# An mLSTM cell and a multiplicative feed-forward block: the third group's output tiles as two pairs by seven products, and other places for folded sums and kept halves

## The chip, the cores and the metric

The kernel runs on one core of a Trainium2 chip. The metric is the device time of one execution in microseconds (us). The engines are named as the profile names them: PE (TensorE; PEld is its weight load), DVE (VectorE), ACT (ScalarE), POOL (GpSimd) and SP (SyncE, whose queue issues most DMAs; ACT's queue issues the output DMAs).

## What is computed

The first block is a recurrent cell. For every batch (4), head (8) and time step (768) a 40 x 40 state is decayed, gets an outer product of v and k, and is read with q:

```
C = f_stab * C + i_stab * outer(v_t, k_t);   n = f_stab * n + i_stab * k_t
y_t = sigmoid(o_t) * (C q_t) / max(|n . q_t|, 1)
```

Its output, put in rows of 320 (8 heads x 40) for 3072 tokens, is x of the second block:

```
h = ((x @ w1) * (x @ w2)) @ w3        # w1, w2: 320 x 1024, w3: 1024 x 1024
out = h @ w_out                        # w_out: 1024 x 320
```

All is float32.

## The kernel before, in words

w3 and w_out are folded: the kernel computes `w3o = w3 @ w_out` once (`w3_mm`), so that a token needs two up products (x w1 and x w2), their elementwise product `ab` (1024 long), and one down product `ab @ w3o`. The raw w3 pieces are made into float32 in buffers `w3` (`convert`, L249), turned, and multiplied with `wo`, which holds w_out. After the last `w3_mm` (step 16) the words of `wo` are free.

The work is cut into 24 units of 128 time steps of one batch (NU = 24), and the main loop runs steps s = 0 to 31. Step s does the cell of unit s (`quarter_work`, s <= 24): PE's records `cell<-v_all,pw`, `cell<-state,qT`, `cell<-qT,kT`, `cell<-vw,kbuf`, in two accumulator tiles `cell[0]` and `cell[1]` (L75), each of two banks. DVE, ACT and POOL make the unit's rows y out of it (DVE L427 to L454, ACT L434, POOL L332, L310 and the state's decay L337). Four units make a group of 512 tokens; there are six groups, 0 to 5.

- Up products of groups 0 to 2 are made plainly (`up`, `up_rest`, steps 2 to 15) into two `ab` tiles per group, out of a rotating pool of six.
- Up products of groups 3 to 5 are made in twelve "late blocks" (`up_by_seven`, one a step, steps 19 to 30): a 2 x 2 product by seven multiplications instead of eight. Its order is `single` and `shared` (PE records `pa`, `pb`, then banks p15 and p67, which in steps 19 to 24 are `cell[1]` and `cell[0]`), later `left` (`pa<-xT,wr`, ahead of the cell's own matmuls), later `product`. ACT empties p15 into four "kept" quarters for each of the two factors j (L710, L712), DVE adds p67 to them (L692, L694, 256 columns each), POOL adds two and two of them (L719), then DVE adds the four blocks `pa`, `pb` to the kept quarters (L692, L694, 512 columns each) and POOL multiplies the factors into `ab` (L737). The kept quarters lie in `wo` (`aside`, L657). The last block does POOL's part on DVE.
- Down products are made in two ways. `ffn_out` makes one tile of 128 tokens whole: 8 matmuls of 320 columns, one ACT copy into `o_sb` (L749), one DMA (L751). `out_by_seven` makes a pair of tiles by seven products of 160 columns with 4 matmuls each (28), in four accumulators o15, o67, o23, o4; it needs sums of the weights, T1 to T4 (`out_weight_sums`, L761, on POOL), and sums of `ab`, S1 to S4 (`ab_sums`, L776, on DVE), and puts the products together with ACT (L798, L800) and DVE (L805 to L811). A matmul in float32 leaves two records in the profile.

The order of the down products is a list written out by hand: group 0's tiles 0 and 1 whole in step 16; the pairs (0,1) and (1,0) in step 17 and (1,1) in step 18 (`pairs_by`); group 2's four tiles whole, one in each of steps 19 to 22; group 3's first two tiles whole in steps 23 and 24; all other pairs (3,1) to (5,1) from step 27 on (`n_out`). In steps 19 to 24 a whole tile is accumulated in `cell[1]`, after `shared` and before `left`. The weight sums T are made twice: at step 16 into `wo`, for the pairs of steps 17 and 18, and again in steps 24 and 25 into `v_all`, `gates` and `q_all`, since the kept quarters overwrite them in `wo` in between.

PE's order is the order in which the program issues matmuls (`in_order`, L84). The other engines run their instructions in the order of issue; the tile framework adds the waits between engines from what each instruction reads and writes.

Of the kernel before, what the change touches and what calls it, by code (L numbers as in the profile page):

```python
# [8 lines left out]
FP = mybir.dt.float32  # L9
U32 = mybir.dt.uint32  # L10
AF = mybir.ActivationFunctionType
OP = mybir.AluOpType
# [4 lines left out]
def kernel(  # L17
# [212 lines left out]


    w3T_t = {}
    turned_w3, ready_w3 = [], []
# [5 lines left out]
    def convert():  # L239
        if not scaled:  # L240
            scale_next()
        dst, raw, ko, half = scaled.pop(0)
        if dst is not None:
            to_f32(dst, raw, nc.vector if dst.shape[-1] == CW else nc.gpsimd)
            return
        w3 = wst.tile([128, CW], FP, name="w3", tag="w3")
        to_f32(w3, raw, nc.vector)
        if half == 0:
            w3T_t[ko] = wst.tile([128, FO, 128], FP, name="w3T", tag="w3T")  # L249
        nc.vector.transpose(out=w3T_t[ko].rearrange("c k (m r) -> c m k r", r=32)[:, 2 * half:2 * half + 2],  # L250
                            in_=w3.rearrange("r (m c k) -> r m k c", m=2, k=FO))
        if half:
            turned_w3.append(ko)
# [369 lines left out]

    ab_t = {}

    def up(gr, fs, cs):


        if gr not in ab_t:
            ab_t[gr] = [ffn.tile([128, FO, 2 * P], FP, name="ab", tag="ab", bufs=6) for _ in range(2)]  # L630
        x, n = x_t[gr], cs.stop - cs.start
        pa, pb = mps([128, len(fs), n], "pa"), mps([128, len(fs), n], "pb")
        for p, wt in ((pa, w1), (pb, w2)):
            for i, f in enumerate(fs):
                for cc in range(KF):
                    mm(p[:, i, :], wt[:, cc, f * 128:(f + 1) * 128], x[:, cc, cs], start=(i == cc == 0), stop=False)
        return pa, pb, x, gr, fs, cs
# [18 lines left out]
    S_t, T_t = {}, {}  # L656
    aside = wo.rearrange("p f d -> p (f d)")  # L657

# [17 lines left out]
    def up_by_seven(gr, f, bank, aside_by):  # L676
# [3 lines left out]
        (B11, B12), (B21, B22) = ([x[:, cc, i * TH:(i + 1) * TH] for i in range(2)] for cc in range(KF))  # L680
        block, kept = {}, [aside[:, j * 4 * TH:(j + 1) * 4 * TH].rearrange("p (i t) -> p i t", i=4) for j in range(2)]
        lo, hi = (ffn.tile([128, 2, TH], FP, name="a_sb", tag="a_sb") for _ in range(2))
# [20 lines left out]
        def shared():  # L703
            p15, p67 = [bank(2 + j) for j in range(2)], [bank(j) for j in range(2)]
            for j in range(2):
                mm(p15[j][:, 0], of(j, 0, 0), B11, stop=False)
                mm(p15[j][:, 1], sum_of(j, 0), T[0], start=False)
            for j in range(2):
                if j:
                    nc.scalar.copy(out=kept[j][:, 0:4:3], in_=p15[j])  # L710
                else:
                    nc.scalar.mul(out=kept[j][:, 0:4:3], in_=p15[j], mul=UP ** -2)  # L712
            for j in range(2):
                mm(p67[j][:, 0], sum_of(j, 1), T[1], stop=False)
                mm(p67[j][:, 1], sum_of(j, 2), T[2], start=False)
            for j in range(2):
                for i in range(2):
                    add(j, kept[j][:, 1 + i], p67[j][:, i], kept[j][:, i])
                aside_by.tensor_tensor(out=kept[j][:, 1:4:2], in0=kept[j][:, 1:3],  # L719
                                        in1=kept[j][:, 3:4].to_broadcast([128, 2, TH]), op=OP.add)  # L720

        def left():
            if gr not in ab_t:
                ab_t[gr] = [ffn.tile([128, FO, TH], FP, name="ab", tag="ab", bufs=6) for _ in range(2)]
            for t in range(2):
                for i in range(2):
                    for j, e in quarters:
                        c0 = (f + i * FH) * 128 + e * L
                        mm(block[j][t][halves[e], i], wr[halves[j], c0:c0 + L], x[halves[j], KF, t * TH:(t + 1) * TH],
                           start=False, stop=(i == 1))  # L730
            for j, dst in enumerate(((lo, hi), [t[:, f:FO:FH, :] for t in ab_t[gr]])):
                add(j, dst[0], block[j][0], kept[j][:, 0:3:2])
                add(j, dst[1], block[j][1], kept[j][:, 1:4:2])

# [20 lines left out]

    def out_weight_sums(places):

        (B11, B12), (B21, B22) = ([w3o[:, k * KH:(k + 1) * KH, i * NH:(i + 1) * NH] for i in range(2)] for k in range(2))
        T1, T2, T3, T4 = T_o[:] = [m[:, i * KH * NH:(i + 1) * KH * NH].rearrange("p (f n) -> p f n", n=NH) for m, i in places]
        for dst, p, q in ((T1, B12, B11), (T2, B22, T1), (T3, B22, B12), (T4, B21, T2)):  # L760
            yield nc.gpsimd.tensor_tensor(out=dst, in0=p, in1=q, op=OP.subtract)  # L761

    T_o, S_o = [], {}
    wsums = out_weight_sums(((v_all, 0), (gates, 0), (gates, 1), (q_all, 0)))

    def quarters_of_ab(gr, j):
        return [[ab_t[gr][j][:, k * KH:(k + 1) * KH, t * P:(t + 1) * P] for k in range(2)] for t in range(2)]

    def ab_sums(gr, j, mem=None):
        mem = mem or [t.rearrange("p h d -> p (h d)") if j == 0 else io.tile([P, H, L], FP, name="pw", tag="pw", bufs=5)  # L770
# [3 lines left out]
        for dst, p, q, op in ((S1, A21, A22, OP.add), (S2, S1, A11, OP.subtract), (S3, A11, A21, OP.subtract),  # L774
                              (S4, A12, S2, OP.subtract)):
            nc.vector.tensor_tensor(out=dst, in0=p, in1=q, op=op)  # L776

    def out_by_seven(gr, j, rows=None):

# [9 lines left out]
        def products(pairs, name):  # L789
            po = mps([P, len(pairs), NH], name)  # L790
            for i, (a, b) in enumerate(pairs):
# [3 lines left out]

        p15 = products(((A11, B11), (S1, T1)), "o15")
        if whole:
            nc.scalar.copy(out=o2[:, 0:4:3], in_=p15)  # L798
        for i in () if whole else range(2):
            nc.scalar.copy(out=o[3 * i], in_=p15[:, i])  # L800
        p67 = products(((S2, T2), (S3, T3)), "o67")
        p23 = products(((A12, B21), (S4, B22)), "o23")
        p4 = products(((A22, T4),), "o4")
        for i in range(2):
            nc.vector.tensor_tensor(out=o[1 + i], in0=p67[:, i], in1=o[i], op=OP.add)  # L805
        if whole:
            nc.vector.tensor_tensor(out=o2[:, 1:4:2], in0=o2[:, 1:3], in1=o2[:, 3:4].to_broadcast([P, 2, NH]), op=OP.add)
        for p, q in () if whole else ((1, 1), (3, 2)):
            nc.vector.tensor_tensor(out=o[p], in0=o[q], in1=o[3], op=OP.add)
        nc.vector.tensor_tensor(out=rows[0], in0=p23.rearrange("p i n -> p (i n)"), in1=rows[0], op=OP.add)  # L810
        nc.vector.tensor_tensor(out=o[2], in0=p4[:, 0], in1=o[2], op=OP.add)  # L811
        for t in range(2):
            t0 = (2 * j + t) * S + gr * P
            leaving.append((out[t0:t0 + P, :], rows[t]))
        if whole:
            leave()

    leaving = []

    def leave():  # L820
        while leaving:
# [4 lines left out]
           for f in range(0, FO, 2)]  # L826
    downs = [(0, 0), (0, 1)] + [(2, j) for j in range(GT)] + [(3, 0), (3, 1)]
    pairs_by = {17: [(0, 1), (1, 0)], 18: [(1, 1)]}
# [4 lines left out]
    n_seven = [0] * 19 + [1] * 12 + [0]  # L833
    n_down = [0] * 16 + [2] + [0] * 2 + [1] * 6 + [0] * 7
    n_out = [0] * 27 + [1, 0, 1, 0, 3]
# [8 lines left out]
    for s in range(len(n_up)):  # L844
# [35 lines left out]
        if s == 16:  # L880
            for _ in out_weight_sums([(aside, i) for i in range(4)]):
                pass
            ab_sums(0, 1, [ffn.tile([128, 2, TH], FP, name="a_sb", tag="a_sb").rearrange("p i t -> p (i t)") for _ in range(2)] +
                    [wst.tile([128, CW], FP, name="w3", tag="w3") for _ in range(2)])
        if s == 17:
# [5 lines left out]
        for x in pairs_by.get(s, ()):  # L891
            if x == (1, 0):
                mem = ffn.tile([128, FO, TH], FP, name="ab", tag="ab", bufs=6)
                ab_sums(1, 1, [mem[:, i * 2:i * 2 + 2].rearrange("p i t -> p (i t)") for i in range(4)])
            out_by_seven(*x, [wst.tile([128, CW], FP, name="w3", tag="w3")[:, 0:DM] if x == (1, 0) else
                              ffn.tile([P, DM], FP, name="o_sb", tag="o_sb", bufs=2) for _ in range(2)])
        if s >= len(n_up) - 2:
            ab_sums(*summed.pop(0))
        def pairs():
            for i in range(n_out[s]):  # L900
                out_by_seven(*outs.pop(0))
                if summed and n_out[s] > 1:
# [11 lines left out]
        if NY < s < NU and s not in pairs_by:  # L914
            if s < NU - 1:
                weights(s + 1)
            out_gate(s)
        if seven and s <= NU:
            ffn_out([downs.pop(0) for _ in range(n_down[s])], [cell[1][:, i, 0:DM] for i in range(2)])
# [53 lines left out]
        with tc.issue_after(gated.ins) if gated else nullcontext():  # L973
            if seven:
                seven[3]()
            for _ in range({NU: 1, NU + 1: 3}.get(s, 0)):
                next(wsums)
            if s == NU + 1:
# [98 lines left out]
```

## Time and profile before

| | us |
|---|---|
| runs of the kernel (3) | 419.91, 423.56, 425.32; median 423.56 |
| the profiled execution | 419.57, of which span 417.7 |
| PE busy | 407.5 |
| DVE busy | 311.5 |
| ACT busy | 182.9 |
| POOL busy | 183.3 |

Busy times by stretch of the profiled execution, from the windows of the trace:

| stretch (us) | steps | PE | DVE | ACT | POOL |
|---|---|---|---|---|---|
| 213.7 to 231.3 | pairs of 17 | 17.60 | 14.46 | 6.47 | 5.02 |
| 231.3 to 242.8 | 18 | 11.50 | 9.40 | 5.18 | 6.28 |
| 242.8 to 256.9 | 19 | 14.10 | 9.62 | 6.12 | 5.80 |
| 256.9 to 271.1 | 20 | 14.20 | 10.82 | 6.22 | 8.40 |
| 271.1 to 285.2 | 21 | 14.10 | 10.65 | 6.22 | 7.88 |
| 285.2 to 299.3 | 22 | 14.10 | 12.08 | 6.21 | 7.89 |
| 326.8 to 351.5 | 25 to 27 | 24.22 | 22.94 | 3.84 | 18.62 |

How to read the lines: the page gives each engine's busy time and share, and 40 equal slices whose digit is the busy share in tenths (PEclk: the clock granted to PE). A timeline line is the start, the duration, engine, line of the kernel, operation, what is written from what, shapes, how often; a bracket gives the idle time ahead and what ended it. A line of waits gives the waiting instruction, what it waited for, the sum, how often, and the longest. Lines of the chain are start, duration and what ran.

### The profile page before, as it was taken

The page shows a single profiled execution, that of the slowest core. Times are in us where ns is not written, and L with a number is a line of the kernel's source. Part 1 is how long each engine was busy: PE and PEld are TensorE (multiplying, and loading weights), DVE is VectorE, ACT ScalarE, POOL GpSimd, SP SyncE. Part 2 cuts the span into 40 slices and gives each one's busy share as a digit, 9 for nine tenths or more (in the row PEclk, how much of TensorE's full clock was granted, in tenths as well). Part 3 has the DMA queues.
Part 4 walks back from the last instruction along what each step waited for, and adds up shares of the span by engine and source line. Part 5 has one row for each costly group of instructions (what it writes and reads, how often), then busy time and mean ns, then how long its engine had stood idle before and what let it go on. Part 6 is the DMA issues. An engine that isn't in the chain of part 4 may idle for free.

```text
span 417.7 us, 13157 instructions
## 1 busy us (share of the span) xinstructions
PE 407.5 (98%) x5351; PEld 337.3 (81%) x5351; DVE 311.5 (75%) x587; ACT 182.9 (44%) x526; POOL 183.3 (44%) x237
## 2 busy tenths in 40 slices
PE   7999899999999989999999999999999999999997
PEld 4768688888788877888789988778778778888896
DVE  6767967668977856869889786778875798575971
ACT  4787756558643844843842452354312211111000
POOL 4533773442302302308971443765544496642100
PEclk9999999999999999999999999999999999999999
DMA  8989987788995584843415487753221010000001
GB/s 189 229 158 193 196 192 128 176 186 182 203 198 140 97 188 130 153 94 61 92 47 118 121 156 148 126 107 82 53 54 39 33 24 31 2 2 31 2 33 63
DMA packets 125291, 46.56 MB, mean 111 GB/s; under 512 B 104816, under 2 KB 116400, under 8 KB 125232
## 3 DMA queue, kind: packets, MB, share of 16 engines
q1 hardware_dynamic: 121632, 41.70, 49.5%
q10 hardware_dynamic: 3600, 4.03, 2.8%
q8 instruction: 42, 0.69, 0.7%
q14 instruction: 17, 0.14, 0.1%
HBM read 39.91 MB, written 5.80 MB: 109 GB/s over the span
## 4 chain that ended last, share of the span: by engine, by line
PE 85%; DVE 4%; DMA 3%; SPq 3%; issue 2%; ACT 1%; POOL 0%; DVEq 0%; ACTq 0%; POOLq 0%
PE pa L92 21%; PE cell L92 20%; PE pb L92 14%; PE o L92 14%; PE wp L92 8%; PE p L92 3%; PE po L92 2%; DMA o_in<-in_o_gate_dram 2%; DMA w3o<-in_moe_w_dram 1%; SPq L136 1%; SPq L186 1%; PE px L95 1%; PE pt L95 1%; DVE pw L776 1%; DVE ab L692 1%
## 5 line engine op out<-in xcount | busy, mean ns | idle before, releaser
L337 POOL TENSOR_TENSOR state<-state,decay 128x164 f32<-128x164 f32 x40 | 22.4, 561 | 118.7 <-DVE state L406 97.5
L92 PE MATMUL pa<-xT,w 128*128 128x256 f32 x240 | 60.6, 383 | 0.0
L92 PEld LDWEIGHTS pa<-xT,w 128*128 128x128 f32 x240 | 44.4, 190 | 6.6 <-POOL w L202 0.4
L305 ACT ACTIVATE pw<-pw,aT 128x64 f32<-128x64 f32 x184 | 46.4, 337 | 2.7 <-DVE pw L297 1.9
L92 PE MATMUL pb<-xT,w 128*128 128x256 f32 x192 | 45.9, 381 | 1.1 <-POOL w L202 1.0
L92 PEld LDWEIGHTS pb<-xT,w 128*128 128x128 f32 x192 | 36.3, 190 | 7.0 <-POOL w L202 2.3
L737 POOL TENSOR_TENSOR ab<-ab,a_sb 128x512 f32<-128x512 f32 x22 | 29.4, 1356 | 27.3 <-DVE ab L692 27.3
L647 DVE TENSOR_TENSOR ab<-pb,a_sb 128x512 f32<-128x512 f32 x24 | 16.5, 690 | 32.2 <-ACT a_sb L646 32.0
L719 POOL TENSOR_TENSOR wo<-wo 128x512 f32<-128x512 f32 x22 | 27.4, 1269 | 28.8 <-DVE wo L694 28.8
L92 PE MATMUL pa<-xT,wr 64*64 64x256 f32 x384 | 37.0, 386 | 0.2 <-POOL wr L202 0.2
L92 PE MATMUL pb<-xT,wr 64*64 64x256 f32 x384 | 36.4, 380 | 0.0
L646 ACT ACTIVATE a_sb<-pa 128x512 f32<-128x512 f32 x24 | 14.3, 595 | 49.7 <-PE pb L92 49.7
L310 POOL TENSOR_SCALAR_AFFINE_SELECT pw<-pw 64x512 f32<-64x512 f32 x48 | 33.3, 694 | 5.9 <-ACT pw L305 4.3
L92 PE MATMUL wp<-wo,w3T 128*128 128x320 f32 x128 | 35.6, 433 | 0.0
L434 ACT COPY h<-cell 64x164 f32<-64x164 f32 x56 | 16.2, 289 | 41.3 <-DVE y L427 40.8
L92 PEld LDWEIGHTS pa<-xT,wr 64*64 64x64 f32 x384 | 18.9, 132 | 15.1 <-issue 8.4
L92 PEld LDWEIGHTS wp<-wo,w3T 128*128 128x128 f32 x128 | 23.8, 190 | 9.0
L92 PE MATMUL cell<-w3o,ab 128*128 128x320 f32 x96 | 26.8, 432 | 0.0
L694 DVE SCALAR_TENSOR_TENSOR a_sb<-pa,wo 128x512 f32<-128x512 f32 x12 | 8.3, 690 | 22.7 <-PE pa L92 22.7
L92 PEld LDWEIGHTS cell<-w3o,ab 128*128 128x128 f32 x96 | 18.3, 190 | 6.9
L92 PEld LDWEIGHTS pb<-xT,wr 64*64 64x64 f32 x384 | 20.1, 133 | 3.0
L92 PE MATMUL o<-w3o,ab 128*128 128x160 f32 x136 | 21.5, 302 | 0.5 <-DVE wo L694 0.5
(222 smaller groups left out, 935.9 us busy)
## 6 DMA issues: line engine op xcount, KB each, us to landing
raw<-in_moe_w_dram SPq DMA_DIRECT2D x64, 128.0 KB, 3.3
kbuf<-in_k_dram SPq DMA_DIRECT2D x24, 160.0 KB, 4.8
v_all<-in_v_dram SPq DMA_DIRECT2D x24, 160.0 KB, 4.5
o_in<-in_o_gate_dram SPq DMA_DIRECT2D x24, 160.0 KB, 4.9
pw<-U_d SPq DMA_DIRECT2D x28, 128.0 KB, 3.9
raw<-in_moe_w_out_dram SPq DMA_DIRECT2D x8, 320.0 KB, 5.0
out_dram<-o_sb ACTq DMA_DIRECT2D x12, 160.0 KB, 3.9
yb<-y_d SPq DMA_DIRECT2D x36, 48.0 KB, 2.9
```

The lines of the kernel that those rows point to most:

```text
L92: in_order(nc.tensor.matmul(out, lhsT=lhsT, rhs=rhs, start=start, stop=stop))
L95: in_order(nc.tensor.transpose(out, in_, ident[0:n, 0:n]))
L136: nc.sync.dma_start(out=dst, in_=rows(src, n))
L305: nc.scalar.activation(out=pw[:, h, :], in_=src[:, h, :], func=AF.Exp, bias=aT[:, c, b * H + h:b * H + h + 1])
L310: nc.gpsimd.affine_select(out=pw[r], in_=pw[r], compare_op=OP.is_ge, fill=0.0, base=0, pattern=[[0, H], [1, L]], channel_multiplier=-1)
L337: nc.gpsimd.tensor_tensor(out=new, in0=old, op=OP.mult, in1=decay[:, b * NP:(b + 1) * NP, 2 * c + x:2 * c + x + 1] .to_broadcast([P, NP, D1]))
L434: nc.scalar.copy(out=h[halves[x], 0:H // 2] if x == e else h[halves[x], H // 2:H], in_=ph[x][halves[e]])
L646: nc.scalar.mul(out=a_sb, in_=pa, mul=UP ** -2)
L647: nc.vector.tensor_tensor(out=ab_t[gr][j][:, fs[0]:fs[-1] + 1, t0:t0 + a_sb.shape[-1]], in0=pb, in1=a_sb, op=OP.mult)
L694: nc.vector.scalar_tensor_tensor(out=out, in0=p, scalar=UP ** -2, in1=q, op0=OP.mult, op1=OP.add)
L719: aside_by.tensor_tensor(out=kept[j][:, 1:4:2], in0=kept[j][:, 1:3], in1=kept[j][:, 3:4].to_broadcast([128, 2, TH]), op=OP.add)
L737: aside_by.tensor_tensor(out=t[:, f:FO:FH, :], in0=t[:, f:FO:FH, :], in1=a, op=OP.mult)
```

## The change

1. The weight sums T1 to T4 are made once, at step 16, into `wo`, and stay there. The second making (four POOL instructions in steps 24 and 25) is gone.
2. The kept quarters of the first factor lie in the two former `w3` buffers, now one tile `w3_mem`; those of the second factor lie in the rows of `ab` in which the block ends, and are overwritten in place. ACT's copy of the second factor's p15 becomes two copies of 256 columns, and POOL's two kept sums of 512 columns become four of 256.
3. The six `ab` tiles are fixed: groups 0 to 5 use (0,1), (2,3), (4,5), (2,3), (4,1), (5,0).
4. Group 2's four whole tiles become the pairs (2,0) and (2,1) by seven products, each in two halves: o15 and o67 in steps 19 and 21, o23 and o4 in steps 20 and 22, in the banks of `cell[1]`, where the whole tile was. The DVE sums of a half stand after DVE's adds of p67 and ahead of `left`'s sums.
5. The S sums of (2,0) and (1,1) are made on POOL in step 17 after the pair (0,1) (those of (1,1) were made on DVE), in the tiles of group 0; those of (2,1) on POOL in step 19.

```diff
+    w3_mem = wst.tile([128, 2 * CW], FP, name="w3", tag="w3", bufs=1)
...
-        w3 = wst.tile([128, CW], FP, name="w3", tag="w3")
+        w3 = w3_mem[:, half * CW:(half + 1) * CW]
...
+    ab_mem = [ffn.tile([128, FO, 2 * P], FP, name=f"ab{i}", tag=f"ab{i}", bufs=1) for i in range(6)]
+    ab_t = {gr: [ab_mem[i] for i in of] for gr, of in enumerate(((0, 1), (2, 3), (4, 5), (2, 3), (4, 1), (5, 0)))}
...
+        kept = [[w3_mem[:, i * TH:(i + 1) * TH] for i in range(4)],
+                [ab_t[gr][i % 2][:, f + i // 2 * FH] for i in range(4)]]
...
-            for j in range(2):
-                if j:
-                    nc.scalar.copy(out=kept[j][:, 0:4:3], in_=p15[j])
-                else:
-                    nc.scalar.mul(out=kept[j][:, 0:4:3], in_=p15[j], mul=UP ** -2)
+            nc.scalar.mul(out=w3_mem.rearrange("p (i t) -> p i t", i=4)[:, 0:4:3], in_=p15[0], mul=UP ** -2)
+            for i in range(2):
+                nc.scalar.copy(out=kept[1][3 * i], in_=p15[1][:, i])
...
-                aside_by.tensor_tensor(out=kept[j][:, 1:4:2], in0=kept[j][:, 1:3],
-                                        in1=kept[j][:, 3:4].to_broadcast([128, 2, TH]), op=OP.add)
+                for p, q in ((1, 1), (3, 2)):
+                    aside_by.tensor_tensor(out=kept[j][p], in0=kept[j][q], in1=kept[j][3], op=OP.add)
...
-            for j, dst in enumerate(((lo, hi), [t[:, f:FO:FH, :] for t in ab_t[gr]])):
-                add(j, dst[0], block[j][0], kept[j][:, 0:3:2])
-                add(j, dst[1], block[j][1], kept[j][:, 1:4:2])
+            at = [[w3_mem.rearrange("p (i t) -> p i t", i=4)[:, t:4:2] for t in range(2)],
+                  [ab[:, f:FO:FH, :] for ab in ab_t[gr]]]
+            for j, dst in enumerate(((lo, hi), at[1])):
+                for t in range(2):
+                    add(j, dst[t], block[j][t], at[j][t])
...
-wsums = out_weight_sums(((v_all, 0), (gates, 0), (gates, 1), (q_all, 0)))
...
-    def out_by_seven(gr, j, rows=None):
+    def out_by_seven(gr, j, rows=None, bank=None):
...
+        if bank:
+            yield first_sums(first())
+            yield second_sums(*second())
+        else:
+            p67 = first()
+            p23, p4 = second()
+            first_sums(p67)
+            yield second_sums(p23, p4)
...
-    downs = [(0, 0), (0, 1)] + [(2, j) for j in range(GT)] + [(3, 0), (3, 1)]
+    downs = [(0, 0), (0, 1), (3, 0), (3, 1)]
...
-    n_down = [0] * 16 + [2] + [0] * 2 + [1] * 6 + [0] * 7
+    n_down = [0] * 16 + [2] + [0] * 6 + [1] * 2 + [0] * 7
...
+            if x == (0, 1):
+                ab_sums(2, 0, in_ab(1), nc.gpsimd)
+                ab_sums(1, 1, in_ab(0), nc.gpsimd)
...
+        if s in (19, 21):
+            halved = out_by_seven(2, (s - 19) // 2, [out_row() for _ in range(2)], lambda name: cell[1][:, int(name in ("o67", "o4")), 0:DM]
+                                  .rearrange("p (i n) -> p i n", n=NH))
+        if s in range(19, 23):
+            next(halved)
+        if s == 19:
+            ab_sums(2, 1, in_ab(0), nc.gpsimd)
...
-            for _ in range({NU: 1, NU + 1: 3}.get(s, 0)):
-                next(wsums)
```

In the new `out_by_seven`, `first()` issues o15, ACT's copies and o67; `second()` issues o23 and o4; `first_sums` is the former L805 to L809, `second_sums` the former L810 and L811 and the row's two DMAs, which leave at the end of the step.

## The prediction

> **What bounds the kernel now.** First the page's busy table and its 40 slices:
> ```profile
> span 417.7 us, 13157 instructions
> PE 407.5 (98%) x5351; PEld 337.3 (81%) x5351; DVE 311.5 (75%) x587; ACT 182.9 (44%) x526; POOL 183.3 (44%) x237
> PE   7999899999999989999999999999999999999997
> PEclk9999999999999999999999999999999999999999
> ```
> TensorE (PE) is busy 98% of the span at full clock. So time comes off by issuing less PE work, and goes back on wherever PE waits for a bank of accumulators. Second, PE's own waits: in the late part there is one above 0.2 us.
> ```profile
> PE o L92 <- DVE wo L694: 0.5, 1, 0.5
> ```
> Third, PE's timeline, for the price of both ways to make output tiles: step 16 (two tiles whole), step 17 (pairs by seven products), step 22 (one tile):
> ```profile
> 204.95 8.78 PE L92 MATMUL po<-w3o,ab 128*128 128x320 f32 x32
> 215.91 1.25 PE L92 MATMUL o<-w3o,ab 128*128 128x160 f32 x8
> 217.00 2.34 PE L92 MATMUL o<-wo,a_sb 128*128 128x160 f32 x16
> 291.36 4.47 PE L92 MATMUL cell<-w3o,ab 128*128 128x320 f32 x16
> ```
> The chain of waits, which merges such runs, says it without the pipelined tail:
> ```profile
> 205.12 8.61 PE po L92 x32
> 233.16 7.80 PE o L92 x56
> 371.41 7.61 PE o L92 x56
> ```
> Two tiles whole take 8.61 to 8.62 us (32 records of 0.269), a pair by seven takes 7.61 (56 of 0.136). Halving the columns halves the time of a record, so seven products in place of eight pay in full. Fourth, the timelines of DVE and POOL where the change puts work:
> ```profile
> 293.98 0.42 DVE L674 TENSOR_TENSOR w3T<-xT,w3T 128x256 f32<-128x256 f32 x1
> 294.31 0.88 DVE L694 SCALAR_TENSOR_TENSOR wo<-cell,wo 128x256 f32<-128x256 f32 x2
> 296.97 0.69 DVE L694 SCALAR_TENSOR_TENSOR a_sb<-pa,wo 128x512 f32<-128x512 f32 x1 [0.99 <-PE pa L92]
> 301.39 0.67 DVE L447 TENSOR_TENSOR h<-y,h 128x328 f32<-128x328 f32 x1 [0.66 <-ACT h L434]
> 235.45 0.64 POOL L337 TENSOR_TENSOR state<-state,decay 128x164 f32<-128x164 f32 x1 [14.10 <-DVE state L406]
> 240.64 0.81 POOL L674 TENSOR_TENSOR w3T<-xT,w3T 128x256 f32<-128x256 f32 x1
> 340.53 2.03 DVE L776 TENSOR_TENSOR pw<-ab 128x512 f32<-128x512 f32 x1
> ```
> The bracket is the idle time ahead. In step 22 DVE rests only 0.99 us before its block sums; POOL stands idle 14.10 us in step 17; L776, 0.69 us when alone, takes 2.03 beside POOL's L761; and L447, 0.50 when alone, takes 0.67 beside L737.
>
> **The change, part by part.** Durations are of the one profiled execution: 419.57 us, span 417.7. It lies 3.99 under the median of the runs, 423.56, so I add that difference at the end.
>
> *Third group as two pairs.* Out go four tiles of 16 records, 4 x 4.31 = 17.24 us; in come 2 x 56 records, 2 x 7.61 = 15.22. Gain 2.02 us, on PE, which is the path. By steps: 19 and 21 keep their length (32 x 0.136 = 4.35 for 4.31), 20 and 22 lose 1.05 us (24 x 0.136 = 3.26).
>
> *Second set of folded weight sums.* Four L761 on POOL go (1.79 + 2.00 + 1.99 + 1.99 = 7.8 us, at 329.9 and 340.0 to 345.9). POOL is off the path, but the last two hold L776 of 340.53 and 342.48 at 2.03 instead of 0.69: 2.7 us on DVE just ahead of the L694 at 347.24 that PE waits for at 348.17. Against that, the third block sum now overwrites what POOL's four kept sums read, so at 336.35 DVE waits for all four, to about 334.43 + 3.0 = 337.4: 1.05 later. Net 1.6 us earlier, so the 0.48 us wait goes: gain 0.48. Next late there is nothing; PE runs on without a gap.
>
> *Kept halves.* Per late block ACT copies 2 x 256 columns for one of 512. An estimate from the copy of 160 columns (0.23) and of 512 (0.58) is 0.3 each, so 0.1 more. In steps 19 to 22 they end about 0.2 after p67 may begin, and PE reaches cell[1][1] only two microseconds later, with o67: nothing. POOL does four sums of 256 for two of 512. The nearest row, L674 on POOL, is 0.73 to 0.81: four spanned 3.0 us, for 2.49. The kept sums for left() are ready 0.5 later; at 295.3 + 3.0 = 298.3 they still meet the third block sum, which began at 298.44. Nothing on PE.
>
> *Sums of (2,0), (1,1) in step 17, on POOL.* They wait for the last read of (0,1)'s tile, about 223.6. Eight at the rows L667 (same shape, 1.27 to 1.72, mean 1.43) end at 235.0, before L337 can start at 235.45. Queued behind are that state, vw, the masks and the token sums, which end at 241.45 with T4 read by PE at 243.30: 1.85 us of slack. At 1.72 each the eight end at 237.4, 1.9 late, and PE loses 0.1. I take 0, the mean being nearest. DVE loses four L776 here (2.61 us).
>
> *Sums of (2,1) in step 19, on POOL.* They stand after the kept sums, 251.3 + 3.0 = 254.3, and take 4 x 1.43 = 5.7, to 260.0. Behind them waits L337 for DVE's state at 260.12: just in time. But they run beside the new DVE sums, next.
>
> *New sums on DVE, before left()'s sums.* First half: two L805 (0.68) and two L809 (0.69 alone, 1.15 beside POOL at 240.47); second half: L810 (0.48) and L811 (0.32). PE's cell matmuls now wait for these to empty cell[1], where ACT did it in 0.42.
> - Step 19: o67 ends near 253.4; 0.68 and 1.15 put the first L694 at 255.3 for 254.46. PE needs its bank at 256.91, has it at 256.0; the chain through L427 and ACT's h ends 0.6 later, against 0.5 to 1.0 of slack at p15. Bounds 0 and 1.2 (both L809 waiting out a POOL sum of 1.36); I take 0.3.
> - Step 20: PE is 1.05 us earlier and POOL's kept sums, which were late already (266.10), end at 269.1 to 269.6; the third block sum still ends before PE wants the bank at 271.4. Step 21 like 19, beside shorter POOL sums. Together 0 to 0.6; I take 0.1.
> - Step 22: the kept adds end at 295.99, behind four token sums L674. L810 and L811 follow to 296.8, later if step 21 left DVE behind (0.5 us). Before, cell matmuls began at 297.53; now they are due at about 296.4. PE waits 0.4 to 0.9; bounds 0 and 1.4; I take 0.7.
>
> *Queues.* Two output DMAs of a pair leave from ACT's queue at the ends of steps 20 and 22, behind the h copies, instead of one in each of four steps. The row buffers are next written two steps later and the landing took 3.9 us: nothing. SP's order does not change, and cutting the pairs into steps adds no instruction. The last block's kept sums move from two L719 on DVE (0.69 each) to four of 256 (0.42): 0.3 us in a stretch where PE's next operands are made 3 us ahead.
>
> *Sum.* -2.02 - 0.48 + 0.3 + 0.1 + 0.7 = -1.4 us, so 418.2 for an execution like the profiled one, and 422.2 beside the median. All waits at their lower bounds give -2.5 (421.1), at the upper ones -2.5 + 1.2 + 0.6 + 1.4 + 0.1 = +0.8 (424.4).
>
> **One rule weighed.** L776 at 2.03 beside a POOL instruction of 1.99, but L447 at only 0.67 for 0.50 beside L737, say that DVE sums from SBUF sometimes wait out a POOL instruction and sometimes hardly lose. The Trainium skill's page "SBUF — State Buffer", section "SBUF: two separate sides", is stricter: a DVE operation with two SBUF inputs and a GpSimd operation reading SBUF take an exclusive lock on shared ports for a whole instruction, and the loser blocks fully. By that rule the third rival below would be the forecast; the row of L776 agrees, that of L447 does not clearly.
>
> **The rivals.**
> 1. *All sums hidden* (421.1): for it, DVE rests 2.0 to 2.5 us before its block sums in steps 19 to 21; against it, 0.99 in step 22 while PE's stretch there shrinks by 1.05.
> 2. *DVE sets the pace of steps 19 to 22* (slower). Place: PE's first cell matmul of each step, waiting for the pair's sums behind the kept adds. Price, if nothing is hidden: 2 x (0.68 + 1.15) + 2 x 0.80 = 5.3 us, against 2.5 gained: +2.8, or 426.4. It decides once these waits pass 2.5 us together. For it: DVE is busy 10.6 to 12.1 of 14.1 us in these steps. Against: three of them have rest to spare.
> 3. *The lock bites*: each two-input DVE sum in steps 19 and 21 waits out a POOL sum. Step 19 then costs 1.2, step 21 0.5, with 0.7 in 22 and 0.1 in 20: 2.5 together, so 423.6, no change.
> 4. *POOL late into step 18*: at L761's 2.0 each the eight sums end at 239.6, 4.2 late, PE waits 2.3 for T4: -1.4 + 2.3 = +0.9, or 424.5. Against: L761 has 640 columns, not 512.
> 5. *The change does not shorten PE's work*: if each short record took its weight load's 0.190 us, a pair would be 10.6 and the whole 2 x (10.6 - 8.62) = +4.0, less 0.48: 427.1. The pairs of steps 17 and 18 rule it out nearly.
>
> **How the numbers follow.** Forecast 0.50, all hidden 0.17, DVE's pace 0.10, the lock 0.15, POOL late 0.05, no shortening 0.03. Cases of both signs are near each other; the forecast's own range is 421.1 to 424.4. The runs of one kernel spread from 419.91 to 425.32, 3.7 below and 1.8 above their median, which widens that to 417.4 and 426.2; the slower rival at 426.4 is let in: 417.5 to 427. A measurement of this kernel tells about 2% (8.5 us) from no change; no case reaches it, so faster 0.02, same 0.92, slower 0.06, the small ones for what I have not seen.
>
> **What would show it.** Right: PE's cell records for the third group number 56 per pair in 7.6 us; no L761 after step 16; no PE wait at the o products of step 27; PE waiting for the o_sb sums in step 22 for under 1 us. Wrong: PE waits on o_sb sums in all four steps (rival 2), a wait for w3T at step 19's start (rival 4), or L809 in step 19 near 1.3 each (rival 3).

## The result and the profile after

The changed kernel takes 425.82 us (median of 22 runs, 423.50 to 429.51); the kernel before, in the same rounds, 421.18 (22 runs, 418.63 to 425.32). The ratio is 1.0117, 95% interval 1.009 to 1.0144: 1.2% slower, inside the 2% but clear of 1. The prediction was 0.3% faster (-1.4 us); its own range ended at +0.8, and only three of its rivals, with chances of 0.10, 0.05 and 0.03, lay beyond that. The profiled execution took 423.62 us, 4.05 more than that of before. Ratios, here and below, leave out executions in a slow state: one of run e5, one of run e7 and two of the kernel before in those rounds.

The page of the kernel after, busy times and slices:

```profile
span 421.9 us, 13293 instructions
PE 407.7 (97%) x5399; PEld 340.4 (81%) x5399; DVE 315.9 (75%) x597; ACT 183.3 (43%) x538; POOL 197.8 (47%) x267
PE   7999899999999999999998999999999999999997
PEclk9999999999999999999999999999999999999999
```

PE is idle for 14.2 us of the span where it was idle for 10.2: the loss is waiting. Its busy time is as before (407.5) although the change takes work away, as PE is busy longer, too, in the steps with waits: from 216.67 to 236.27 us, the step 17 of the table below, for 17.70 us, in the same step before for 17.18. POOL has 14.5 us more to do. One slice of PE in the middle, the 22nd, fell below 9. PE's waits, kernel after, from 196 to 335 us, give the places (before there was none in these steps, and one of 0.5 us later, at the o products of step 27):

```profile
PE o L92 <- DVE o_sb L807: 1.9, 1, 1.9
PE cell L92 <- ACT o_sb L799: 1.2, 2, 0.6
PE cell L92 <- issue: 0.9, 1, 0.9
PE cell L92 <- ACT h L435: 0.6, 1, 0.6
PE cell L92 <- DVE state L417: 0.3, 1, 0.3
```

The wait of 0.5 is gone, as foreseen; five others have come. (The one for `issue` is in a stage before the change's.) To size them I take a step's length as the time between the first PE records of it and of the next, from PE's timeline. A step begins with its feed-forward products and ends with its cell matmuls; the last column runs from step 25 to the end of PE's last record.

| kernel | 17 | 18 | 19 | 20 | 21 | 22 | 23 | 24 | after 24 |
|---|---|---|---|---|---|---|---|---|---|
| before | 17.18 | 9.68 | 14.14 | 14.16 | 14.14 | 14.13 | 14.14 | 13.34 | 87.82 |
| after | 19.60 | 9.68 | 15.20 | 14.49 | 15.02 | 13.52 | 14.23 | 13.35 | 87.07 |
| difference | +2.42 | 0 | +1.06 | +0.33 | +0.88 | -0.61 | +0.09 | +0.01 | -0.75 |

Step 17 began 0.76 us later (216.67 for 215.91); in the runs below its start scatters from 214.7 to 218.6 us. With that, this is the 4.2 us of span.

**Step 17.** The timelines of POOL and DVE, kernel after, while (0,1) and (1,0) are multiplied:

```profile
222.07 1.90 POOL L774 TENSOR_TENSOR ab<-ab 128x512 f32<-128x512 f32 x1
222.15 0.69 DVE L774 TENSOR_TENSOR xT<-ab 128x512 f32<-128x512 f32 x1
222.88 1.64 DVE L774 TENSOR_TENSOR xT<-xT,ab 128x512 f32<-128x512 f32 x1
224.05 1.60 POOL L774 TENSOR_TENSOR ab<-ab,ab 128x512 f32<-128x512 f32 x1
224.45 1.76 DVE L774 TENSOR_TENSOR xT<-ab 128x512 f32<-128x512 f32 x1
225.62 1.71 POOL L774 TENSOR_TENSOR ab<-ab 128x512 f32<-128x512 f32 x1
226.13 1.75 DVE L774 TENSOR_TENSOR w3T<-ab,xT 128x512 f32<-128x512 f32 x1
227.29 1.71 POOL L774 TENSOR_TENSOR ab<-ab,ab 128x512 f32<-128x512 f32 x1
227.80 0.67 DVE L807 TENSOR_TENSOR o_sb<-o,o_sb 128x160 f32<-128x160 f32 x2
```

POOL's sums of (2,0) begin at 222.07, while PE is still at work on (0,1). Three of DVE's four sums of (1,0) take 1.64 to 1.76 us for the 0.69 of the first. They stand ahead of L807, which empties the bank that PE wants next; it starts at 227.80, and PE has stood still for 1.90 us when it goes on:

```profile
228.52 2.44 PE L92 MATMUL o<-wo,xT 128*128 128x160 f32 x16 [1.90 <-DVE o_sb L807]
```

The step is 2.42 us longer: 1.90 of idle time and 0.52 more of busy time. Before, L805 (now L807) stood at 223.93 and there was no gap:

```profile
223.33 0.69 DVE L776 TENSOR_TENSOR w3T<-ab,xT 128x512 f32<-128x512 f32 x1
223.93 0.68 DVE L805 TENSOR_TENSOR o_sb<-o,o_sb 128x160 f32<-128x160 f32 x2
224.61 3.42 PE L92 MATMUL o<-wo,xT 128*128 128x160 f32 x24
```

**Steps 19 to 22.** PE's timeline of the first half of (2,0) in step 19 and the second in step 20, kernel after, with the bracket of idle time:

```profile
252.09 1.25 PE L92 MATMUL cell<-w3o,ab 128*128 128x160 f32 x8
253.18 1.25 PE L92 MATMUL cell<-wo,ab 128*128 128x160 f32 x8
255.01 2.44 PE L92 MATMUL cell<-wo,ab 128*128 128x160 f32 x16 [0.58 <-ACT o_sb L799]
```

```profile
268.70 2.34 PE L92 MATMUL cell<-w3o,ab 128*128 128x160 f32 x16
270.88 1.25 PE L92 MATMUL cell<-wo,ab 128*128 128x160 f32 x8
```

The work came out as forecast: 32 records, then 24, in place of two tiles of 16 wide ones. But o67 waits for ACT's two copies of o15, although it writes the other bank of the cell tile. And DVE's sums beside POOL, in step 19:

```profile
257.69 1.28 POOL L774 TENSOR_TENSOR ab<-ab 128x512 f32<-128x512 f32 x1
258.26 2.24 DVE L811 TENSOR_TENSOR o_sb<-o_sb 128x160 f32<-128x160 f32 x2
259.04 1.28 POOL L774 TENSOR_TENSOR ab<-ab,ab 128x512 f32<-128x512 f32 x1
260.42 0.68 DVE L695 SCALAR_TENSOR_TENSOR a_sb<-pa,w 128x512 f32<-128x512 f32 x1
```

Two small sums take 2.24 us, and behind them the block sums L695 and, further on, the operands h and state of step 20 come late (0.6 and 0.3 us in the list of waits). L695, which reads PSUM, takes 0.68 beside the same POOL sums.

The granted clock matters to the median: in the profiled execution it was 1.0, but 17 of the 22 executions show a mean of 0.996 or less. Those 17 have a median of 426.04, the other five one of 424.43.

### The profile page after: what moved, and what is told of

Its sections match the earlier page's. It is cut to its first block, busy times and chain, and to the rows that moved or that the text cites. A ratio compares the mean times of both kernels' runs of the same rounds, so it can differ in the third digit from the quotient of the medians.

```text
span 421.9 us, 13293 instructions
## 1 busy us (share of the span) xinstructions
PE 407.7 (97%) x5399; PEld 340.4 (81%) x5399; DVE 315.9 (75%) x597; ACT 183.3 (43%) x538; POOL 197.8 (47%) x267
## 4 chain that ended last, share of the span: by engine, by line
PE 82%; issue 4%; SPq 4%; POOL 3%; DVE 3%; DMA 3%; ACT 1%; POOLq 0%; DVEq 0%; ACTq 0%
PE pa L92 21%; PE cell L92 17%; PE pb L92 14%; PE o L92 12%; PE wp L92 8%; PE p L92 5%; DMA w3o<-in_moe_w_dram 3%; SPq L136 2%; POOL wo L760 1%; PE px L95 1%; SPq L186 1%; POOL ab L774 1%; PE pt L95 1%; PE po L92 1%; DVE xT L774 1%
## 5 line engine op out<-in xcount | busy, mean ns | idle before, releaser
L719 POOL TENSOR_TENSOR w<-w 128x256 f32<-128x256 f32 x22 | 16.0, 728 | 34.0 <-DVE w L695 30.3
L333 POOL TENSOR_TENSOR vw<-v_all,wT 128x328 f32<-128x328 f32 x24 | 18.6, 777 | 7.0 <-DMA v_all<-in_v_dram 5.3
L92 PEld LDWEIGHTS o<-w3o,ab 128*128 128x128 f32 x136 | 19.3, 190 | 1.1 <-issue 0.8
L695 DVE SCALAR_TENSOR_TENSOR a_sb<-pa,w 128x512 f32<-128x512 f32 x12 | 8.2, 687 | 15.0 <-PE pa L92 14.5
```

Of the source, the lines that this page charges most:

```text
L92: in_order(nc.tensor.matmul(out, lhsT=lhsT, rhs=rhs, start=start, stop=stop))
L333: nc.gpsimd.tensor_tensor(out=vw_t[n], in0=vbuf[n % NBV], op=OP.mult, in1=wT[:, c, b * H:(b + 1) * H].unsqueeze(2).to_broadcast([P, H, D1]))
L719: aside_by.tensor_tensor(out=kept[j][p], in0=kept[j][q], in1=kept[j][3], op=OP.add)
```

## Experiments

Theory A: the loss is (1) POOL's sums of (2,0) beside DVE's sums of (1,0) in step 17, (2) o67's wait for ACT's copies in steps 19 and 21, (3) POOL's sums of (2,1) beside L811 in step 19; the kept halves and the single set of weight sums cost nothing. Rivals are named with each run. Step lengths of all runs, in us:

| run | 17 | 18 | 19 | 20 | 21 | 22 | 23 | 24 | after 24 |
|---|---|---|---|---|---|---|---|---|---|
| e1_kept_only | 17.18 | 9.67 | 14.15 | 14.16 | 14.13 | 14.14 | 14.13 | 13.35 | 87.07 |
| e2_reversed | 17.18 | 9.67 | 15.03 | 14.07 | 15.01 | 13.53 | 14.22 | 13.35 | 87.07 |
| e3_copy_after | 22.02 | 9.67 | 14.68 | 14.49 | 14.17 | 13.94 | 14.23 | 13.34 | 87.07 |
| e4_no_sums_21 | 20.67 | 9.67 | 15.03 | 13.12 | 15.02 | 13.47 | 14.23 | 13.35 | 87.07 |
| e5_reversed_and_copy_after | 17.18 | 9.67 | 14.68 | 14.49 | 14.17 | 13.93 | 14.22 | 13.34 | 87.07 |
| e6_sums_21_on_dve | 17.18 | 9.68 | 14.41 | 14.42 | 14.17 | 13.96 | 14.22 | 13.34 | 87.07 |
| e7b_sums_21_in_two_halves | 17.18 | 9.68 | 14.18 | 13.58 | 14.17 | 14.45 | 14.22 | 13.34 | 87.07 |
| e8_sums_l811_later | 17.17 | 9.68 | 14.18 | 14.85 | 14.27 | 14.08 | 14.23 | 13.35 | 87.07 |
| e9_token_sums_later | 17.18 | 9.68 | 14.18 | 13.52 | 14.26 | 13.78 | 14.96 | 13.35 | 87.07 |
| e10_filler_in_the_wait | 19.60 | 9.68 | 15.29 | 14.48 | 15.02 | 13.47 | 14.22 | 13.35 | 87.07 |

**The first two parts alone.** Kept halves and single weight sums as in the change; the third group whole, and the sums of (1,1) on DVE, as before.

```diff
-    downs = [(0, 0), (0, 1), (3, 0), (3, 1)]
+    downs = [(0, 0), (0, 1)] + [(2, j) for j in range(GT)] + [(3, 0), (3, 1)]
...
-            if x == (0, 1):
-                ab_sums(2, 0, in_ab(1), nc.gpsimd)
-                ab_sums(1, 1, in_ab(0), nc.gpsimd)
+            if x == (1, 0):
+                ab_sums(1, 1, in_ab(0))
...
-        if s in range(19, 23):
-            next(halved)
-        if s == 19:
-            ab_sums(2, 1, in_ab(0), nc.gpsimd)
```

> The change without its pairs: weight sums stay in w_out's words, kept halves in w3's buffers and in place, but the third group's four tiles are made whole, one a step, as before, and the sums of (1,1) are on DVE as before. Theory A (the loss is in the pairs' surroundings: step 17's sums on POOL, and steps 19 to 22): steps 17 to 24 as long as in the kernel before (17.18, 9.68, 14.14, 14.16, 14.14, 14.13, 14.14, 13.34 us between PE's first records), the stretch from step 25 to the end 0.8 us shorter as in the changed kernel (90.1 for 90.9), ratio to before 0.998. Rival B (the split copies and sums of the kept halves cost): some of steps 19 to 24 longer by 0.1 to 0.5 each, ratio 1.002 to 1.008.

Measured: 419.85 us (10 runs), ratio 0.997, interval 0.9942 to 0.9997. Steps 17 to 24 stand as before, the rest is 0.75 shorter. These two parts are worth their gain; everything lost comes with the pairs of group 2 and the sums on POOL.

**The order of the destinations.** S1 of (2,0) goes to the last rows of the tile instead of the first.

```diff
-                ab_sums(2, 0, in_ab(1), nc.gpsimd)
+                ab_sums(2, 0, in_ab(1)[::-1], nc.gpsimd)
```

> The changed kernel, with the four sums of (2,0) laid into their tile in the opposite order, so that the first one overwrites what the pair (0,1)'s last product reads and POOL can't begin before that product ends. Theory A (in step 17 POOL's sums began at 222.07, beside DVE's sums of (1,0), which took 1.64 to 1.76 us for 0.69, so that PE waited 1.90 us for L807): POOL begins after 224, three of DVE's four L774 back at 0.7, PE's wait of 1.9 gone, step 17 at 17.2 to 17.6 us for 19.60, all else as in the changed kernel; time 2.0 to 2.4 us under it. Rival (DVE's sums L811, still beside POOL, hold PE as well): step 17 above 18.5.

Measured: 421.51 us (10 runs), ratio 1.0014, interval 0.9978 to 1.0049. Timelines of this kernel:

```profile
223.12 0.68 DVE L774 TENSOR_TENSOR w3T<-ab,xT 128x512 f32<-128x512 f32 x1
223.56 1.36 POOL L774 TENSOR_TENSOR ab<-ab 128x512 f32<-128x512 f32 x1 [2.42 <-PE o L92]
223.72 0.67 DVE L807 TENSOR_TENSOR o_sb<-o,o_sb 128x160 f32<-128x160 f32 x2
224.41 3.42 PE L92 MATMUL o<-wo,xT 128*128 128x160 f32 x24
224.50 1.96 DVE L811 TENSOR_TENSOR o_sb<-o_sb 128x160 f32<-128x160 f32 x2
```

POOL now does wait (2.42 us) for PE's last reads of the tile, so DVE's four sums are through at 0.68 or 0.69 each, and step 17 is back at 17.18: all of its 2.42 us. L811 is still stretched to 1.96, and PE does not notice. So it is what stands ahead of L807 that counts. The first rows of the tile are read by the first product only, which PE was done with at about 217.9 in the changed kernel: that is where the prediction's start of 223.6 failed. Here POOL does start at 223.56, and then the sums cost nothing, as the prediction had it.

The median is about 4.3 us under the changed kernel's (by the ratios), more than the 2.0 to 2.4 expected. The step lengths account for 3.0 of it: L811 of step 19 happens to take 1.64 us here for 2.24, and steps 19 and 20 are 0.17 and 0.42 shorter, which was not foreseen. The rest goes along with the clock: 3 of 10 executions are at 0.996 or less, for 17 of 22.

**The copies behind o67.** In the halved pairs ACT's copies L799 are issued after the o67 products.

```diff
             p15 = products(((A11, B11), (S1, T1)), "o15")
+            p67 = products(((S2, T2), (S3, T3)), "o67") if bank else None
...
-            return products(((S2, T2), (S3, T3)), "o67")
+            return p67 or products(((S2, T2), (S3, T3)), "o67")
```

> The changed kernel, with ACT's two copies of o15 issued after the products o67 in the halves of steps 19 and 21, so that o67 no longer waits for them. Theory A (o67 waits 0.58 us twice for a copy that reads another bank of the same tile): both waits of PE on L799 gone; step 21 at 14.4 to 14.6 us for 15.02; step 19 shorter by 0.3 to 0.6, or not at all if DVE's sums, which now wait for the copies too, hold the next step. Rival (the copies only uncover another wait): steps 19 and 21 as long as before this edit, 15.2 and 15.0.

Measured: 424.72 us (10 runs), ratio 1.0093, interval 1.0059 to 1.0128. Both waits for L799 are gone; step 21 is 0.85 shorter, step 19 0.52, while step 22 gave 0.42 back. What is left of the loss in step 19 (14.68 for 14.14) is a wait of 0.42 for L695, behind the stretched L811, at the start of step 20. This execution also met a slower clock in step 17. PE's timeline (L808 is L807 of the other runs), then windows (time, PE, PEld, DVE, ACT, POOL, PEclk, DMA share, GB/s):

```profile
227.61 4.07 PE L92 MATMUL o<-wo,xT 128*128 128x160 f32 x16 [2.94 <-DVE o_sb L808]
```

```profile
226.60:227.60 1.00, 0.00 (x0) 0.00 (x0) 0.92 (x3) 0.00 (x0) 1.00 (x1) 0.97 0.42 66
227.60:229.00 1.40, 1.39 (x5) 1.40 (x6) 1.31 (x2) 0.00 (x0) 1.32 (x2) 0.50 0.59 101
229.00:230.90 1.90, 1.90 (x9) 1.90 (x8) 1.24 (x3) 0.00 (x0) 1.90 (x3) 0.50 0.52 144
231.00:232.00 1.00, 1.00 (x9) 1.00 (x9) 0.22 (x1) 0.00 (x0) 0.96 (x1) 1.00 0.00 0
```

Here all four of DVE's sums met POOL, PE waited 2.94 us, and from the end of that wait on the granted clock was 0.50 for some 3.4 us; the 16 records took 4.07 us for 2.44.

**Without POOL's sums of (2,1).** The pair (2,1) uses the sums of (2,0), so 256 rows of the output are other numbers; nothing else is left out.

```diff
         if s == 19:
-            ab_sums(2, 1, in_ab(0), nc.gpsimd)
+            S_o[2, 1] = S_o[2, 0]
```

> The changed kernel without the four sums of (2,1) on POOL in step 19; the second pair uses the sums of the first, so its 256 output rows are not the reference's. Theory A (these sums stretch DVE's L811 to 2.24 us, and PE pays 1.0 to 1.1 us at the start of step 20, in waits on L695, ACT's h and L417): L811 at 0.7 to 1.2, step 20 at 13.2 to 13.5 for 14.49, step 19 shorter by 0.2. Rival C (DVE's pair sums themselves, not POOL, hold PE): step 20 above 14.0.

Measured: 423.86 us (10 runs), ratio 1.0085, interval 1.0052 to 1.0117. L811 is alone again, and step 20 has its whole gain (13.12 for 14.49); step 19 is 0.17 shorter:

```profile
259.87 0.68 DVE L811 TENSOR_TENSOR o_sb<-o_sb 128x160 f32<-128x160 f32 x2
```

In step 17 PE waited 2.94 us here too, and the clock stayed at 1.00.

**Both edits of e2 and e3 together.**

> The destinations of step 17's sums in reversed order, and the copies L799 of the halved pairs issued behind the o67 products: the two edits tried alone, now together. Theory A (the two costs are independent, one in step 17, one 0.58 us wait each in steps 19 and 21): step 17 about 17.2 us on PE as before the change, step 19 about 14.7, step 20 14.1 to 14.5, step 21 about 14.2, step 22 about 13.9, the tail after step 24 about 87.07. Against the kernel before (steps 19 to 22 together 56.57, tail 87.82) that is +0.4 to +0.8 and -0.75, so a ratio of 0.999 to 1.001. Rival B (the 0.58 us is slack that DVE's stretched L811 takes anyway): steps 19 to 22 as with the reversal alone, 57.6 together, ratio 1.0014.

Measured: 420.66 us (12 runs), ratio 1.0003, interval 0.9975 to 1.0031. The step lengths are those of the two edits put side by side (Theory A). Steps 19 to 22 still sum to 57.27 for 56.57 before.

**The sums of (2,1) on DVE,** at the end of step 18, in addition to both edits.

```diff
-        if s == 19:
-            ab_sums(2, 1, in_ab(0), nc.gpsimd)
...
+            if s == 18:
+                ab_sums(2, 1, in_ab(0))
             if NY <= s - 2 < NU:
```

> As the run with both edits, and the four sums of (2,1) made by DVE at the end of step 18, where it waits 1.04 us for yb, instead of by POOL in step 19. Theory A (POOL's sums cost by stretching DVE's L811 from 0.68 to 2.24 us for the pair; DVE has room for four more of 0.69): step 19 about 14.45, step 20 about 13.1 as in the run without these sums, steps 21 and 22 about 14.2 and 13.5 to 13.9, ratio 0.995 to 0.997. Rival B (DVE has no room: 2.76 us less the 1.04 us idle make its L695 in step 19 1.7 us late, and PE waits for it): step 19 or 20 0.8 to 1.7 us longer than that, ratio 0.998 to 1.001.

Measured: 420.81 us (12 runs), ratio 1.0003, interval 0.9981 to 1.0025. Rival B held: DVE's L428 starts 1.59 us after step 20 does, against 0.28 without these sums (e4), and PE waits 0.49 for h and 0.30 for state there. The cost is DVE's lateness, whoever brings it about.

**POOL's sums of (2,1) two by two,** in the gaps of steps 18 and 20, in addition to both edits.

```diff
-        if s == 19:
-            ab_sums(2, 1, in_ab(0), nc.gpsimd)
...
+            if s == 18:
+                late = sums_of_ab(2, 1, in_ab(0), nc.gpsimd)
+            if s in (18, 20):
+                next(late), next(late)
```

> As the run with both edits, and POOL makes the sums of (2,1) two at a time: two at the end of step 18, where it waits 3.23 us for DVE's L407, and two in step 20 behind its L736, when DVE is about to turn blocks, which read one tile. Theory A (what costs is only that POOL's sums meet DVE's L811): L811 about 0.68 to 1.2 us for the pair, step 19 about 14.45, step 20 about 13.1, steps 21 and 22 about 14.2 and 13.5 to 13.9, ratio 0.995 to 0.997. Rival B (the sums meet DVE's other sums of two tiles there, L448 and L454 in step 20, and delay POOL's own L333 and L338): step 19 or 20 0.5 to 1.5 us longer, ratio 0.998 to 1.000.

> The kernel with POOL's sums of (2,1) in two halves once more, for a profile at the full clock: its earlier profiled execution ran all the way at a granted clock of 0.56. Its other eleven executions were not faster than the kernel before, so Rival B of that run is now expected: L811 is no longer stretched (0.68 to 1.2 us for the pair), but step 19 or step 20 is 0.5 to 1.5 us longer than the 14.45 and 13.1 that its removal alone would give, since POOL's L333, L311 and L338 come late.

Measured: 420.33 us (12 runs), ratio 1.0004, interval 0.9974 to 1.0033; the second profile 419.26 in one run. Step 19 (14.18) is about as long as before the change, step 20 (13.58) is 0.58 shorter, and L811 (L816 in this kernel) takes 0.69 for the pair. So step 20 lost 0.48 of its gain, at the edge of what was expected of the second profile; but step 22, of which nothing was expected, takes 14.45 for 13.93 in e5, and more than half of what step 20 gained is gone again. The trace shows how. POOL's second two sums (L778 here) meet DVE's sums of two SBUF tiles:

```profile
273.55 1.52 POOL L778 TENSOR_TENSOR ab<-ab 128x512 f32<-128x512 f32 x1
274.22 0.88 DVE L452 SCALAR_TENSOR_TENSOR den<-den 128x8 f32<-128x8 f32 x1
```

L452 takes 0.88 for 0.35 in e5, and L454 behind it 1.39 for 0.76. DVE carries this lateness along: it starts L428 1.28 us after step 22 does, against 0.75 in e5, and the two sums that empty the halves' banks end 0.5 us later in the step. PE's cell matmuls start 0.1 us behind them in both runs. That is the meeting that Rival B foresaw, with its price in step 22; this is read off the two traces, and no run of its own tested it.

**L811 of (2,0) later,** behind L320 of the next step, in addition to both edits; POOL's sums stay in step 19.

```diff
+            if gr == 2 and j == 0:
+                yield
             for p, q in ((1, 1), (3, 2)):
                 nc.vector.tensor_tensor(out=o[p], in0=o[q], in1=o[3], op=OP.add)
...
+            if s == 19:
+                next(halved)
```

> As the run with both edits (reversed order, copies behind o67), and of the first pair the two sums of DVE that POOL's sums stretched (L811, 2.10 us for two of 0.34) are issued a step's end later, behind DVE's L320, and so out of the way of what PE waits for at step 20's start; POOL's sums of (2,1) stay in step 19. Theory A (what step 20 loses is DVE's lateness of 1.4 us from that pair, nothing else of POOL's): step 19 about 14.45, step 20 13.1 to 13.3, step 21 14.2 to 14.45, step 22 about 13.9, tail 87.07: 1.2 to 1.5 us less than the run with both edits, ratio to before about 0.997. Rival B (DVE is the pace of these steps, wherever its sums stand): step 20 stays at 14.2 to 14.5 and the ratio at 1.000.

Measured: 420.10 us (12 runs), ratio 0.9977, interval 0.9951 to 1.0002. In the profiled execution step 19 is 14.18, but step 20 14.85: there DVE waited 2.58 us for yb (0.70 in the next run), POOL's sums began only at 257.98, and what they met was L448, L452 and, behind them on POOL, the state that PE waits for:

```profile
261.01 1.18 DVE L448 TENSOR_TENSOR h<-y,h 128x328 f32<-128x328 f32 x1 [0.66 <-ACT h L435]
261.80 1.52 POOL L774 TENSOR_TENSOR ab<-ab,ab 128x512 f32<-128x512 f32 x1
262.47 0.88 DVE L452 SCALAR_TENSOR_TENSOR den<-den 128x8 f32<-128x8 f32 x1
```

The next run has the same steps 19 and 20 in its program; there POOL's sums began at 255.26, and step 20 took 13.52. So with L811 out of the way step 20 gets back most of its gain in one of two traces. By these two the gain depends on when a load lands; how often it lands late is not shown.

**The token sums of step 22 later,** behind L816, in addition to that.

```diff
+        if s == 22:
+            token_sums(4)
...
-            if s - 2 in range(5 * GT - 1, NU, GT):
+            if s - 2 in range(6 * GT - 1, NU, GT):
```

> As the run with L811 later, and DVE's four token sums L673 of the fifth group, 1.45 us ahead of L695 and of the halves' sums L815 and L816 in step 22, are issued behind L816. Theory A (step 22 gives back 0.8 of its 1.05 us because DVE reads the halves' banks late, with these four in front): step 22 13.1 to 13.5 instead of 13.9, ratio about 0.996. Rival B (step 22's loss has another source): step 22 stays at 13.9.

Measured: 420.85 us (12 runs), ratio 0.9997, interval 0.9971 to 1.0024. Step 22 is 13.78, not 13.1 to 13.5, and step 23 0.73 longer: the sums moved now meet POOL's L719 and make L695 late instead. A miss: there is no free place for them at the end of that step.

**Filler in the wait of step 17,** the changed kernel otherwise as it is.

```diff
+            for _ in range(8 if (gr, j) == (1, 0) else 0):
+                mm(cell[1][:, 1, 328:456], ident, ident)
```

> The changed kernel as it is, and in step 17, where PE waits 1.90 to 2.94 us for the o67 bank of (1,0), eight products of the unit matrix into columns of a cell tile that nothing reads, about 1.2 us, issued between o15 and o67. Step 17 itself should keep its length (about 19.6 to 20.7 us), as the products lie inside the wait. Theory A (PE's idle time there lowers the granted clock to a half for some 3.4 us in many executions: 17 of the changed kernel's 22 show a mean clock of 0.996 or less, against 3 of 10 with the reversed order, where this wait is gone; and those 17 are 2 us longer): most executions at a clock of 0.999 to 1.0, the median near 424.0, ratio to before about 1.007 to 1.008. Rival B (the clock falls for another reason, or the filled time counts as idle all the same): three quarters of the executions at 0.996 or less, the median 425.5 to 426, ratio 1.011 to 1.012.

Measured: 424.15 us (12 runs), ratio 1.0075, interval 1.0047 to 1.0102. The filler stands in the gap, and step 17 is still 19.60:

```profile
228.40 1.95 PE L92 MATMUL cell<-ident 128*128 128x128 f32 x16
230.46 2.44 PE L92 MATMUL o<-wo,xT 128*128 128x160 f32 x16
```

Only 2 of the 12 executions are at 0.996 or less, against 17 of 22 without it, 7 of 10 and 8 of 10 in the runs e3 and e4, where the wait stood too; in the kernel before, over the rounds of the experiments, it is 28 of 100, and 7 of 17 in this run's own round. In the other runs without the wait it is 2 to 5 of 10 or 12. So the counts are as Theory A has them: the wait costs its length, and in many executions a stretch at half clock besides. The ratio says it less surely, as its interval overlaps that of the changed kernel (1.009 to 1.0144).

The mean clock of an execution doesn't tell where the slow stretch lay. One stretch of 3.4 us at 0.50 lowers the mean of 422 us by 0.004, so 0.996 is about one such stretch (an estimate from e3's windows). Of the traces only e3's shows it behind the wait of step 17. In the profiled execution of this run, and of e6, it lies at 18.6 to 22.0 us; such early stretches would account for the kernel before, but that is not shown.

## Why the prediction was wrong, point by point

- **The step that failed** is the sentence on step 17's sums on POOL: "They wait for the last read of (0,1)'s tile, about 223.6." They wait for the last read of the rows that they overwrite first, and those were free long before; POOL began at 222.07, as soon as its own work before was done. Taken as 0, this cost 2.42 us on PE (undone by the reversal), and in the median some 1.6 us more by the clock, as far as the executions at 0.996 or less differ from the others. The text asked only whether POOL would be done in time (rival 4), not what its start falls beside on DVE.
- **The signs of being right** all came: 56 records a pair, no weight sums after step 16, no wait in step 27, a wait of 0.5 in step 22. None of them looked at step 17.
- **The rule weighed** bit there, where no rival had placed it, and in step 19, where rival 3 had. DVE's L774 at 1.64 to 1.76 us beside POOL's 1.60 to 1.71, and 0.68 with the reversal, are what the Trainium skill's "SBUF — State Buffer", section "SBUF: two separate sides", states: a DVE operation with two SBUF inputs and a GpSimd operation that reads SBUF lock each other out, and the loser waits for a whole instruction. The trace agrees for sums of two SBUF tiles, L811 (2.24 for 0.68) among them; L695, which reads a PSUM bank, kept 0.68 beside the same POOL sums.
- **Third group as two pairs**, -2.02: the work itself is right. Where no wait is left, the first half's step takes 14.18 (e8 and e9; 14.14 before) and the second's 13.12 (e4; 14.16 before): -1.0 a pair. No one run has both.
- **Steps 19 and 21**, taken as +0.3 and next to nothing: +1.06 and +0.88. Most of it is o67's wait for L799, which the text had not seen at all: of o67 it asked only whether the late block's copies would have left its bank by then. The profile shows 0.58 idle; the step loses 0.85 (15.02 for 14.17 in step 21), 0.27 of it as longer busy time. Step 19 has 0.17 more from the stretched L811 (e4); without o67's wait L811 alone costs it 0.50 (14.68 in e5, 14.18 in e8, where L811 stands later).
- **Step 20**, -1.05 and some of 0.1: +0.33 measured, so 1.38 was given back, by POOL's sums of (2,1) (e4). Most of that is L811's stretch: step 20 takes 14.49 with L811 at 2.24, 14.07 at 1.64 (e2) and 13.52 where L811 stands later (e9). The bound of 1.2 for step 19 was near, but the price came due in step 20.
- **Step 22**, +0.7: 0.44 given back. Right in kind, and smaller: the last of DVE's sums of the halves, L815, ends at 302.10, and PE's weight loads for the cell matmuls begin at 302.17, after 0.51 of idle time. The profile doesn't name what ended it; the times fit.
- **Weight sums**, -0.48: -0.75, the wait in step 27 gone and nothing late behind it. The prediction took the idle time alone; PE's busy time from step 25 on fell as well, from 87.34 to 87.06 us. **Kept halves**, nothing: right (e1).

Summed in the prediction's terms, for the profiled execution: -2.1 for the work (-1.05 twice), -0.75, +2.42 in step 17, +1.06 and +0.88 in 19 and 21, +1.38 and +0.44 in 20 and 22, +0.1 in 23 and 24, +0.76 before step 17: +4.2 us. What stays open is how often a late yb undoes e8, and in how many executions the slow clock lies behind step 17. None of the mended pairs beats the first two parts alone (0.997) clearly; that kernel is the version to keep.

## What to carry to other kernels

When work moves to POOL, ask of each instruction which rows its first write waits for, not when the tile is done; then list what DVE does from that moment, and price each sum of two SBUF tiles at POOL's time (here 1.64 to 1.76 us for 0.69). A new user of a bank may wait for a reader of its tile's other bank, as o67 did here for 0.58 us: look for the readers that the program puts between two products on one tile. A wait costs more than the idle time that a profile shows for it (2.42 us for 1.90, 0.85 for 0.58, 0.75 for 0.48). And the clock may fall behind a gap of two or three microseconds in PE's work, as behind the 2.94 us of e3: read the clock of many executions, not of the profiled one alone.

## What was not expected of the hardware

- A gap of 2.94 us halved PE's clock for 3.4 us in one execution (e3) and left it at 1.00 in another (e4). The Trainium skill's "TensorE: Matmul & The Clock Gate", section "Part 1: The HAM clock gate", tells of a free-running window of about 3.4 us, after one idle window of which the clock goes to half. The length of the slow stretch agrees (some 3.4 us in e3). The gaps here, 1.90 to 2.94 us in the profiled executions, are shorter than such a window, and the counts of the last experiment (17 of 22 with the gap, 2 of 12 with 1.95 us of filler in it) say that they lower the clock all the same; the measurement decides.
- One execution of the kernel e7 ran at a granted clock of 0.56 in the mean, from end to end, with a span of 697.6 us. The record doesn't show why.
